# Linear attention into a tanh-shrink MLP on one core: accumulators in one PSUM tile, 1/den of batch 1 spread by TensorE, transposes of batch 2 on TensorE, loads at chunk edges

## The chip, the core and the metric

The kernel runs on one core of a Trainium2 chip. The core's engines work side by side, each with a queue of its own: TensorE (PE, matrix products, with a row of its own in the profile for its weight loads, PEld), VectorE (DVE), ScalarE (ACT), GpSimd (POOL) and SyncE (SP). POOL and SP issue the DMAs here. The metric is the device time of one execution in microseconds (us), the median over runs.

## The reference, cut to what matters

```python
batch, n_heads, seq, head_dim = (8, 8, 576, 64)      # q, k, v
n_tokens, d_model, d_ff = (4608, 512, 2048)          # w_in, w_out

def phi(x):
    return np.where(x > 0, x, np.exp(x) - 1.0) + 1.0
q_p, k_p = (phi(q), phi(k))
kv = np.einsum('bhsd,bhse->bhde', k_p, v)
z = np.sum(k_p, axis=2)
num = np.einsum('bhsd,bhde->bhse', q_p, kv)
den = np.einsum('bhsd,bhd->bhs', q_p, z)[..., None] + 1e-06
attn = (num / den)
x = attn.transpose(0, 2, 1, 3).reshape(B * S, H * D)
h = x @ w_in
g = h - np.tanh(h)
return (g @ w_out)
```

Inputs and output are fp32; products are computed from bf16 with fp32 sums.

## The kernel before

The 4608 tokens are worked on in nine chunks of 512, the loop over `c` at L312. A chunk has two layers. Layer 1 is 16 groups `fi`: four matmuls (`l1mm`, L227) sum one accumulator `h` of 128 x 512, then `l1act` takes a tanh on ACT (L232) and the subtraction on DVE (L233), which writes `gT`. Layer 2 is 16 steps `s` of four matmuls each (`l2mm`, L242) into four accumulators `o`; each, once complete, is copied to SBUF by ACT (L247) and written out by two DMAs on SP (L250). In chunk 0 layer 2 goes over quarters of `gT` first (its four accumulators are open side by side), in all others over accumulators.

Attention is worked on by batch (576 tokens, 8 heads), one batch ahead of the chunk that needs it. Its steps for batch b: load k, q and v by POOL (`load_kq`, `load_v`); `phi` in halves `i`, an exp on ACT (L101) and two operations on DVE (L102, L103), for k (`a_kphi`) and q (`a_qphi`); qT, the transpose of phi(q); the KV products and the sum of k (`a_kv`, 36 matmuls, L142, then a mask on DVE, L146); the denominators (`a_den`, L154 on PE, L158 and L160 on DVE); the spread of 1/den over the 64 rows of each head; the numerators (`num_mm`, L179 and L182) and their product with 1/den, which is x, transposed, in `xT`.

qT is made in two ways. `a_qT_pe` transposes 128 x 128 blocks on PE (L126) and copies them out on ACT and DVE (L130, L132); it serves batches 0 and 1. `a_qT_dma` issues one DMA transpose on SP (L116); it serves the others. 1/den is spread in two ways too. `a_spread` writes it to DRAM (`ds`, four DMAs, L167) and reads it back in broadcast (`rdb`, two DMAs, L170), all on SP; DVE then multiplies numerators in PSUM by `rdb` (`a_num`, L190, L195). It serves batches 1 to 7. For batch 0, `a_num_copy` copies the numerators to SBUF on ACT (L203, L206), `a_spread_pe` spreads 1/den by matmuls with a 0/1 matrix `sel` (L215) into a four-bank accumulator `bp`, and `a_scale` multiplies on DVE (L220).

The order on each engine is that in which the code is written (`manual_schedule`). What of the next batches is put behind which group or step stands in the lists `s1` and `s2` (L315 to L349). Numbers that matter here: in chunk 1, KV of batch 2 behind group 6 and its denominators behind group 15; in chunks 2 to 6, KV behind group 6 and denominators behind group 10; numerators behind steps 9 to 13. Loads of k and q for batch c + 2 are held back by `gate`, a one-element copy on POOL that waits for a group of `gT`: group 11 in chunk 1, group 4 after that.

PSUM is eight banks, handed out by pools: at the start four banks for warm-up and `bp` and four for the rest, from chunk 0 on six (`dps`) for `h` and `o`, and two (`aps`) for attention.

Of the kernel before, what the change touches and what calls it, by code (L numbers as in the profile page):

```python
# [15 lines left out]
def kernel(  # L16
# [27 lines left out]
    opool = ctx.enter_context(tc.tile_pool(name="opool", bufs=5))  # L44
    ctx.enter_context(tc.manual_schedule())

# [73 lines left out]
    def a_qT_pe(b, i, pool, tag):  # L120
        if i == 0:
            new_qT(b)
        for n, (j0, j1) in enumerate(((0, 5), (5, 9))):
            ps = pool.tile([128, 8, 128], BF16, name="tps", tag=tag)
            for j in range(j0, j1):
                nc.tensor.transpose(ps[:, j - j0, :], qp_t[b][:, i, j].rearrange("p h d -> p (h d)"), ident)  # L126
            src = ps[:, 0:j1 - j0, :]
            dst = qT_t[b][:, i, j0:j1].rearrange("p j g t -> p j (g t)")
            if n == 0:
                nc.scalar.copy(dst, src)  # L130
            else:
                nc.vector.tensor_copy(dst, src)  # L132

    def a_kv(b, pool, tag):
        kz_t[b] = work.tile([128, 2, 2, 160], BF16, name="kz")
        kp, vt = kp_t[b], v_b[b % 2]
        ps = [pool.tile([128, 2, 192], F32, name=f"kvps{hg}", tag=tag) for hg in range(2)]
# [10 lines left out]
    def a_den(b, pool, tag):  # L148

        kz, qT = kz_t[b], qT_t[b]  # L150
        ps = pool.tile([128, J, 16], F32, name="denps", tag=tag)
# [6 lines left out]
        nc.vector.tensor_scalar(den, ps.rearrange("p j t -> p (j t)"), 1e-6, None, ALU.add)  # L158
# [16 lines left out]
    def num_mm(b, p, pool, tag):  # L175
        kz, qT = kz_t[b], qT_t[b]
        ps = pool.tile([128, 8, 64], F32, name="numps", tag=tag)
# [8 lines left out]
    def a_num(b, p):  # L186
        rdb = rdb_t[b]
        ps = num_mm(b, p, aps, "aps")
# [10 lines left out]
    def a_num_copy(b, pool, tag):  # L199

        ns = rpool.tile([128, NP, J, 64], F32, name="ns", tag="rdb")
        ps = num_mm(b, NP, pool, tag)
        nc.scalar.copy(ns[:, :, 8, :], ps[:, 0:NP, :])  # L203
        for p in range(NP):
            ps = num_mm(b, p, pool, tag)
            nc.scalar.copy(ns[:, p, 0:8, :], ps)  # L206
# [79 lines left out]
    with tc.tile_pool(name="bpa", bufs=1, space=bass.MemoryType.PSUM) as bpa:  # L286
        with tc.tile_pool(name="sps", bufs=4, space=bass.MemoryType.PSUM) as sps:

            wps = bpa.tile([128, 4, 512], F32, name="wps", tag="bp")
            for n in range(28):  # L290
                nc.tensor.matmul(wps[:, n % 4, :], zero[:, 0:128], zero, start=True, stop=True)
            for i in range(2):
                a_kphi(0, i)
            for i in range(2):
                a_qphi(0, i)
            for i in range(2):
                a_qT_pe(0, i, sps, "sps")
            a_kv(0, sps, "sps")
            a_den(0, sps, "sps")
            ns0 = a_num_copy(0, sps, "sps")  # L300
# [11 lines left out]
    for c in range(NC):  # L312
# [4 lines left out]
        if c == 0:  # L317
            s1[11].append(lambda: a_kphi(1, 0))
# [3 lines left out]
            s2[4].append(lambda: a_qT_pe(1, 0, aps, "aps"))  # L322
            s2[5].append(lambda: a_qT_pe(1, 1, aps, "aps"))
            s2[6].append(lambda: a_kv(1, aps, "aps"))
# [25 lines left out]
        if c == 0:  # L350

            hs = [dps.tile([128, 512], F32, name="h", tag="dps") for _ in range(4)]
# [5 lines left out]
        for fi in range(4 if c == 0 else 0, NF):  # L358
            h = dps.tile([128, 512], F32, name="h", tag="dps")
# [46 lines left out]
```

## Time and profile before

| | |
|---|---|
| three runs | 326.29, 329.56 (median), 329.67 us |
| the profiled execution | 328.22 us |
| its span in the profile | 326.4 us |
| mean granted TensorE clock | 0.961 |
| PE busy, share of the span | 293.0 us, 90% |
| DVE | 180.5 us, 55% |
| ACT | 146.3 us, 45% |
| POOL | 50.6 us, 16% |

The span is what the trace covers; the execution's own time is 1.8 us longer. Times in the views count from the span's start. Busy shares are averages over stages with different limits, so the views to read here are the strip of busy tenths, which shows where PE has holes, PE's waits, which name what ended them, and the chain of waits, which gives the order in time. A granted clock under 1 in a window means that PE ran slower there than it can.

### The profile page before, as it was taken

How to read it: one execution, taken by the hardware profiler on the slowest of the kernel's cores; microseconds unless marked ns; L12 is line 12 of the kernel's file. 1: busy time of each engine (PE TensorE's matmuls, PEld its weight loads, DVE VectorE, ACT ScalarE, POOL GpSimd, SP SyncE). 2: the span in 40 equal slices, each digit the busy share in tenths (PEclk: the TensorE clock that was granted, in tenths of full speed). 3: DMA queues.
4: the chain of work that ended last, by engine and by line, in shares of the span. 5: the costliest groups of instructions: out<-in, count | busy, mean ns of one | idle time of the engine just before them, and what ended most of it. 6: DMA issues, size and time to landing. Idle time of an engine off the chain costs nothing.

```text
span 326.4 us, 4546 instructions
## 1 busy us (share of the span) xinstructions
PE 293.0 (90%) x1698; PEld 138.3 (42%) x1728; DVE 180.5 (55%) x299; ACT 146.3 (45%) x223; POOL 50.6 (16%) x88
## 2 busy tenths in 40 slices
PE   8469999089599999899999998999999999999994
PEld 3334454035233454345444443444454444444441
DVE  5763962069625676557665765586478048405700
ACT  3524842047416456345635562556256126316511
POOL 8924062002300060006000500020000000000000
PEclk9898999759969999999999999999999999999998
DMA  7999999632987678938892979196610730031022
GB/s 113 175 207 202 202 176 171 183 93 35 142 148 180 133 113 138 238 81 128 160 215 66 155 132 241 41 146 167 150 33 4 190 71 15 0 92 38 0 64 64
DMA packets 38901, 40.00 MB, mean 123 GB/s; under 512 B 16768, under 2 KB 33376, under 8 KB 37984
## 3 DMA queue, kind: packets, MB, share of 16 engines
q0 software_dynamic: 17536, 18.35, 35.6%
q1 hardware_dynamic: 21344, 21.37, 29.2%
q8 instruction: 13, 0.21, 0.3%
q14 instruction: 8, 0.07, 0.1%
HBM read 44.96 MB, written 9.57 MB: 167 GB/s over the span
## 4 chain that ended last, share of the span: by engine, by line
PE 65%; DMA 22%; DVE 5%; SPq 2%; issue 2%; ACT 2%; POOL 1%; DVEq 0%; ACTq 0%; POOLq 0%
PE h L227 33%; PE o L242 24%; DMA rdb<-ds 10%; DMA ds<-rden 5%; PE kvps L142 4%; DMA qT<-qp 3%; DMA qraw<-in_q_dram 2%; DMA out_dram<-osb 2%; PE numps L179 2%; DVE rden L160 2%; SPq L167 1%; DVE xT L190 1%; ACT osb L247 1%; PE denps L154 1%; DVE xT L220 1%
## 5 line engine op out<-in xcount | busy, mean ns | idle before, releaser
L242 PE MATMUL o<-w_out_sb,gT 128*128 128x512 bf16 x562 | 132.8, 386 | 1.0 <-issue 0.4
L227 PE MATMUL h<-xT,w_in_sb 128*128 128x512 bf16 x560 | 128.7, 385 | 2.8 <-DVE xT L220 2.0
L233 DVE TENSOR_TENSOR gT<-h,th 128x512 bf16<-128x512 f32 x144 | 97.1, 688 | 55.3 <-ACT th L232 54.7
L232 ACT ACTIVATE th<-h 128x512 f32<-128x512 f32 x144 | 85.2, 598 | 53.6 <-PE h L227 49.9
L242 PEld LDWEIGHTS <-gT 128*128 128x128 bf16 x576 | 56.4, 99 | 83.4 <-issue 20.5
L227 PEld LDWEIGHTS <-w_in_sb 128*128 128x128 bf16 x576 | 56.0, 99 | 70.8 <-issue 6.9
L247 ACT COPY osb<-o 128x512 f32<-128x512 f32 x36 | 21.1, 586 | 108.6 <-PE o L242 83.7
L190 DVE TENSOR_TENSOR xT<-numps,rdb 128x512 bf16<-128x512 f32 x28 | 18.6, 688 | 31.7 <-DMA rdb<-ds 19.7
L179 PE MATMUL numps<-qT,kz 128*128 128x512 bf16 x32 | 12.1, 393 | 14.6 <-DVE xT L190 14.5
L78 POOL DMA_DIRECT2D v<-in_v_dram x32 | 19.3, 638 | 33.9 <-PE kvps L142 25.9
L103 DVE TENSOR_TENSOR kp<-e,r 128x1152 bf16<-128x1152 bf16 x16 | 12.4, 775 | 18.3 <-ACT e L101 17.4
L101 ACT ACTIVATE e<-kraw 128x1152 bf16<-128x1152 bf16 x16 | 18.5, 1161 | 4.5 <-DMA kraw<-in_k_dram 4.5
L101 ACT ACTIVATE e<-qraw 128x1152 bf16<-128x1152 bf16 x16 | 18.4, 1164 | 1.6 <-DMA qraw<-in_q_dram 1.6
L238 POOL COPY g<-gT 1x1 bf16<-1x1 bf16 x5 | 0.9, 178 | 110.7 <-DVE gT L233 110.7
L103 DVE TENSOR_TENSOR qp<-e,r 128x1152 bf16<-128x1152 bf16 x16 | 12.1, 758 | 5.8 <-ACT e L101 4.7
L142 PE MATMUL kvps<-v,kp 64*128 64x192 bf16 x288 | 14.5, 257 | 0.3
L142 PEld LDWEIGHTS <-kp 64*128 64x128 bf16 x288 | 12.5, 100 | 3.4 <-issue 3.2
L63 POOL DMA_DIRECT2D kraw<-in_k_dram x16 | 10.1, 639 | 12.2 <-ACT th L232 9.6
L146 DVE TENSOR_TENSOR kz<-kvps,mask 128x320 bf16<-128x320 f32 (+1 forms) x18 | 7.2, 448 | 5.8 <-PE kvps L142 5.8
L63 POOL DMA_DIRECT2D qraw<-in_q_dram x16 | 10.0, 647 | 2.4 <-issue 2.4
L102 DVE TENSOR_SCALAR r<-kraw 128x1152 bf16<-128x1152 bf16 x16 | 8.0, 503 | 1.9 <-DMA kraw<-in_k_dram 1.9
L160 DVE RECIPROCAL rden<-den 128x144 f32<-128x144 f32 x8 | 8.4, 1053 | 0.3
(36 smaller groups left out, 71.8 us busy)
## 6 DMA issues: line engine op xcount, KB each, us to landing
out_dram<-osb SPq DMA_DIRECT2D x72, 128.0 KB
rdb<-ds SPq DMA_DIRECT2D x14, 576.0 KB
kraw<-in_k_dram POOLq DMA_DIRECT2D x16, 288.0 KB, 5.1
qraw<-in_q_dram POOLq DMA_DIRECT2D x16, 288.0 KB, 7.1
v<-in_v_dram POOLq DMA_DIRECT2D x32, 144.0 KB, 7.6
w_in_sb<-in_moe_w_in_dram POOLq DMA_DIRECT2D x4, 512.0 KB, 8.1
w_out_sb<-in_moe_w_out_dram POOLq DMA_DIRECT2D x4, 512.0 KB, 14.7
ds<-rden SPq DMA_DIRECT2D x28, 4.5 KB
```

The source lines that it names most:

```text
L63: nc.gpsimd.dma_start(out=t[64 * hg:64 * hg + 64].rearrange("p i h j d -> p (i h) (j d)"), in_=src[b, 4 * hg:4 * hg + 4].rearrange("h (p j ...
L78: nc.gpsimd.dma_start(out=v_b[b % 2][64 * hg:64 * hg + 64, i, 0:2].rearrange("p h j d -> p h (j d)"), in_=v[b, h0:h0 + 2].rearrange("h (p ...
L101: nc.scalar.activation(e, x, AF.Exp)
L103: nc.vector.tensor_tensor(store[b][:, i].rearrange("p j h d -> p h j d"), e, r, ALU.min)
L142: nc.tensor.matmul(ps[hg][:, i, :], kp[r, i, j].rearrange("p h d -> p (h d)"), vt[r, i, :, j, :], start=(j == 0), stop=(j == J - 1))
L179: nc.tensor.matmul(ps, kz[:, p // 2, p % 2, 0:128], qT[:, p % 2, 0:8, p // 2, :], start=True, stop=True)
L190: nc.vector.tensor_mul(xT[:, p, S * b:S * b + 512].rearrange("p (j t c) -> p j t c", j=8, t=4), ps.rearrange("p j (t c) -> p j t c", t=4), ...
L227: nc.tensor.matmul(h, w_in_sb[:, p, fi * 128:(fi + 1) * 128], xT[:, p, c * 512:(c + 1) * 512], start=(p == 0), stop=(p == NP - 1))
L232: nc.scalar.activation(th, h, AF.Tanh)
L233: nc.vector.tensor_sub(gT[:, fi, :], h, th)
L242: nc.tensor.matmul(o, gT[:, fi, i * 128:(i + 1) * 128], w_out_sb[:, fi, :], start=(fi == 0), stop=(fi == NF - 1))
L247: nc.scalar.copy(osb, o)
```

## The change

Five things are changed.

1. PSUM is one tile `ps_all` of eight banks. `Banks` gives banks out in a written cycle: 0 to 5 for `h` and `o` (`dense`), 6 and 7 for attention (`attn`), other cycles at the start and in chunk 0, where layer 1 uses all eight and attention uses 4 to 7 in layer 2.
2. The warm-up is 44 matmuls and not 28. At the start both halves of the spread stand ahead of the scales, each with four banks of its own.
3. Batch 1's 1/den is spread on PE: numerators behind step 9 of chunk 0, copied out by ACT, the spread in halves behind steps 11 and 13, each followed by two scales.
4. Batch 2's qT is made on PE, behind groups 5 and 6 of chunk 1. Its phi moves up: k behind steps 14 and 15 of chunk 0, q behind groups 0 and 2 of chunk 1. KV of batch 2 stands behind group 8, its denominators behind group 11. In chunks 2 to 6, KV stands behind group 5 and denominators behind group 8.
5. k and q of batch 3 are loaded behind group 2 of chunk 1, without a gate; those of later batches behind group 0 of their chunk, gated to that group; v behind group 8.

```diff
+    psum = ctx.enter_context(tc.tile_pool(name="psum", bufs=1, space=bass.MemoryType.PSUM))
+    ps_all = psum.tile([128, 8, 512], F32, name="ps_all")
+    class Banks:
+        def __init__(self, order):
+            self.order, self.n = order, 0
+        def __call__(self):
+            self.n += 1
+            return ps_all[:, self.order[(self.n - 1) % len(self.order)], :]
+    dense = Banks([0, 1, 2, 3, 4, 5])
+    attn = Banks([6, 7])
...
-            ps = pool.tile([128, 8, 128], BF16, name="tps", tag=tag)
+            ps = banks().bitcast(BF16).rearrange("p (j t) -> p j t", t=128)
...
-    def a_spread_pe(b, pool, pairs):
+    def a_spread_pe(b, bank0, pairs):
-        bp = pool.tile([128, 4, 512], F32, name="bp", tag="bp")
+        bp = ps_all[:, bank0:bank0 + 4, :]
...
-            for n in range(28):
-                nc.tensor.matmul(wps[:, n % 4, :], zero[:, 0:128], zero, start=True, stop=True)
+    for n in range(44):
+        nc.tensor.matmul(ps_all[:, n % 4, :], zero[:, 0:128], zero, start=True, stop=True)
...
-            bp_a = a_spread_pe(0, bpa, (0, 1))
-        with tc.tile_pool(name="bpb", bufs=1, space=bass.MemoryType.PSUM) as bpb:
-            bp_b = a_spread_pe(0, bpb, (2, 3))
-            for p in range(NP):
-                a_scale(0, p, ns0, (bp_a, bp_b)[p // 2], 144 * (p % 2))
-    dps = ctx.enter_context(tc.tile_pool(name="dps", bufs=6, space=bass.MemoryType.PSUM))
-    aps = ctx.enter_context(tc.tile_pool(name="aps", bufs=2, space=bass.MemoryType.PSUM))
+    bp_a = a_spread_pe(0, 0, (0, 1))
+    bp_b = a_spread_pe(0, 4, (2, 3))
+    for p in range(NP):
+        a_scale(0, p, ns0, (bp_a, bp_b)[p // 2], 144 * (p % 2))
...
+            side = Banks([4, 5, 6, 7])
+            sub = {}
+            def spread1(h):
+                sub["bp"] = a_spread_pe(1, 4, (2 * h, 2 * h + 1))
+                for p in (2 * h, 2 * h + 1):
+                    a_scale(1, p, sub["ns"], sub["bp"], 144 * (p % 2))
...
-            s2[8].append(lambda: (a_den(1, aps, "aps"), a_spread(1)))
-            s2[9].append(lambda: load_v(3))
-            for p in range(NP + 1):
-                s2[min(12 + p, 15)].append(lambda p=p: a_num(1, p))
-            s2[15].append(lambda: a_kphi(2, 0))
+            s2[8].append(lambda: a_den(1, side))
+            s2[9].append(lambda: (sub.update(ns=a_num_copy(1, side)), load_v(3)))
+            s2[11].append(lambda: spread1(0))
+            s2[13].append(lambda: spread1(1))
+            s2[14].append(lambda: a_kphi(2, 0))
+            s2[15].append(lambda: a_kphi(2, 1))
         elif n1 < B:
-            s1[6].append(lambda: a_kv(n1, aps, "aps"))
-            s1[15 if c == 1 else 10].append(lambda: (a_den(n1, aps, "aps"), a_spread(n1)))
+            s1[8 if c == 1 else 5].append(lambda: a_kv(n1, attn))
+            s1[11 if c == 1 else 8].append(lambda: (a_den(n1, attn), a_spread(n1)))
...
-                s1[6].append(lambda: load_v(c + 3))
+                s1[8].append(lambda: load_v(c + 3))
         if c == 1:
-            s1[0].append(lambda: a_kphi(2, 1))
-            s1[2].append(lambda: a_qphi(2, 0))
-            s1[4].append(lambda: (a_qphi(2, 1), a_qT_dma(2)))
+            s1[0].append(lambda: a_qphi(2, 0))
+            s1[2].append(lambda: (a_qphi(2, 1), load_k(3), load_q(3)))
+            s1[5].append(lambda: a_qT_pe(2, 0, attn))
+            s1[6].append(lambda: a_qT_pe(2, 1, attn))
         if c >= 1 and n2 < B:
-            l = 11 if c == 1 else 4
-            s1[l].append(lambda: (gate(gT, l), load_k(n2), load_q(n2)))
-            d = 5 if c == 1 else 2
+            if c > 1:
+                s1[0].append(lambda: (gate(gT, 0), load_k(n2), load_q(n2)))
+            d = 4 if c == 1 else 2
...
-            hs = [dps.tile([128, 512], F32, name="h", tag="dps") for _ in range(4)]
+            hs = [ps_all[:, fi, :] for fi in range(4)]
+            first = Banks([4, 5, 6, 7, 0, 1, 2, 3])
...
-            h = dps.tile([128, 512], F32, name="h", tag="dps")
+            h = first() if c == 0 else dense()
...
-                os_[i] = dps.tile([128, 512], F32, name="o", tag="dps")
+                os_[i] = ps_all[:, i, :] if c == 0 else dense()
```

DVE's rows from the denominators of batch 1, in layer 2 of chunk 0, to the first phi of batch 2. Before:

```order
L158 TENSOR_SCALAR den<-denps 128x144
L160 RECIPROCAL rden<-den 128x144
L190 TENSOR_TENSOR xT<-numps,rdb 128x512 x4
L195 TENSOR_TENSOR xT<-numps,rdb 128x4x64
L102 TENSOR_SCALAR r<-kraw 128x1152
L103 TENSOR_TENSOR kp<-e,r 128x2x9x64
```

And now:

```order
L172 TENSOR_SCALAR den<-ps_all 128x144
L174 RECIPROCAL rden<-den 128x144
L234 TENSOR_TENSOR xT<-ns,ps_all 128x4x9x16 x4
L116 TENSOR_SCALAR r<-kraw 128x1152
L117 TENSOR_TENSOR kp<-e,r 128x2x9x64
```

Five products with `rdb`, which comes from DRAM, are replaced by four scales that read `ns` and the spread in PSUM.

DVE's rows in layer 1 of chunk 1, from the second half of phi(q) of batch 2 on (`gT` rows are the subtractions of layer 1). Before:

```order
L102 TENSOR_SCALAR r<-qraw 128x1152
L103 TENSOR_TENSOR qp<-e,r 128x2x9x64
L233 TENSOR_TENSOR gT<-h,th 128x512 x2
L146 TENSOR_TENSOR kz<-kvps_797,mask 128x320
L146 TENSOR_TENSOR kz<-kvps_798,mask 128x320
L233 TENSOR_TENSOR gT<-h,th 128x512 x9
```

And now:

```order
L116 TENSOR_SCALAR r<-qraw 128x1152
L117 TENSOR_TENSOR qp<-e,r 128x2x9x64
L247 TENSOR_TENSOR gT<-ps_all,th 128x512 x3
L146 COPY qT<-ps_all 128x512
L247 TENSOR_TENSOR gT<-ps_all,th 128x512
```

Two qT copies come in, the first behind three subtractions, the second behind one more. The rows on ACT are alike: tanh of groups 3 to 5 stand between the last exp of q and its first qT copy.

POOL's loads from v of batch 3 to k and q of batch 3. Before:

```order
L78 DMA v_88<-in_v_dram 64x2x576 x4
L78 DMA v_87<-in_v_dram 64x2x576 x4
L238 COPY g_881<-gT 1x1
L63 DMA kraw<-in_k_dram 64x4x576 x2
L63 DMA qraw<-in_q_dram 64x4x576 x2
```

And now, as far as the gate of batch 4's:

```order
L92 DMA v_92<-in_v_dram 64x2x576 x4
L77 DMA kraw<-in_k_dram 64x4x576 x2
L77 DMA qraw<-in_q_dram 64x4x576 x2
L92 DMA v_91<-in_v_dram 64x2x576 x4
L252 COPY g_1043<-gT 1x1
```

k and q of batch 3 move ahead of v of batch 4, and the gate ahead of them is gone; the gate that follows is that of batch 4's k and q.

More of the change, by code (lines that the diff above doesn't have):

```diff
@@ L118, in a_qT_dma, with a_qT_pe @@
             in_=qp_t[b].rearrange("p i j h d -> p (i j h d)"))
-    def a_qT_pe(b, i, pool, tag):
+    def a_qT_pe(b, i, banks):
         if i == 0:
@@ L132, in a_qT_pe, with a_kv @@
                 nc.vector.tensor_copy(dst, src)
-    def a_kv(b, pool, tag):
+    def a_kv(b, banks):
         kz_t[b] = work.tile([128, 2, 2, 160], BF16, name="kz")
         kp, vt = kp_t[b], v_b[b % 2]
-        ps = [pool.tile([128, 2, 192], F32, name=f"kvps{hg}", tag=tag) for hg in range(2)]
+        ps = [banks()[:, 0:384].rearrange("p (i e) -> p i e", i=2) for hg in range(2)]
         for i in range(2):
@@ L146, in a_kv, with a_den @@
                 nc.vector.tensor_mul(kz_t[b][:, hg, i, :], ps[hg][:, i, 0:160], mask[:, hg, i, :])
-    def a_den(b, pool, tag):
+    def a_den(b, banks):
         kz, qT = kz_t[b], qT_t[b]
-        ps = pool.tile([128, J, 16], F32, name="denps", tag=tag)
+        ps = banks()[:, 0:J * 16]
         for n, p in enumerate((0, 2, 1, 3)):
@@ L173, in a_spread, with num_mm @@
         rdb_t[b] = rdb
-    def num_mm(b, p, pool, tag):
+    def num_mm(b, p, banks):
         kz, qT = kz_t[b], qT_t[b]
-        ps = pool.tile([128, 8, 64], F32, name="numps", tag=tag)
+        ps = banks().rearrange("p (j t) -> p j t", j=8)
         if p < NP:
@@ L284 @@
         nc.vector.memset(v_b[i][:, :, 2], 1.0)
[L286 to L307 removed]
+    for n in range(44):
+        nc.tensor.matmul(ps_all[:, n % 4, :], zero[:, 0:128], zero, start=True, stop=True)
+    for i in range(2):
+        a_kphi(0, i)
+    for i in range(2):
+        a_qphi(0, i)
+    first = Banks([4, 5, 6, 7, 0, 1, 2, 3])
+    for i in range(2):
+        a_qT_pe(0, i, first)
+    a_kv(0, first)
+    a_den(0, first)
+    ns0 = a_num_copy(0, first)
+    bp_a = a_spread_pe(0, 0, (0, 1))
+    bp_b = a_spread_pe(0, 4, (2, 3))
+    for p in range(NP):
+        a_scale(0, p, ns0, (bp_a, bp_b)[p // 2], 144 * (p % 2))
     load_k(2)
```

17 lines of the change are left out of this document (9 added, 8 removed).

## The prediction

> **What bounds the kernel now.** I read the page's strip of busy tenths first, then TensorE's (PE's) waits, then the chain of waits in order of time, and last the timeline of the places these name. In the page's two strips, 40 slices of 8.16 us each, the reader is to see that PE is full from the twelfth slice on, and that its holes and its low granted clock lie together in the first third.
>
> ```profile
> PE   8469999089599999899999998999999999999994
> ...
> PEclk9898999759969999999999999999999999999998
> ```
>
> PE's waits (total us, times, longest) name the holes: numerators that wait for VectorE (DVE) to free an accumulator, one of them 10.2 us long; the denominators of batch 2 behind a DMA transpose; transposes at the start.
>
> ```profile
> PE numps L179 <- DVE xT L190: 14.5, 6, 10.2
> PE tps L126 <- DVE qp L103: 4.5, 2, 3.9
> PE denps L154 <- DMA qT<-qp: 3.5, 1, 3.5
> PE h L227 <- DVE xT L220: 2.0, 1, 2.0
> ```
>
> The chain (start, duration, what) gives each chunk's first layer-1 matmul:
>
> ```profile
> 24.49 0.59 PE h L227
> ...
> 69.74 4.25 PE h L227 x14
> ...
> 109.34 6.04 PE h L227 x28
> ...
> 141.54 5.83 PE h L227 x27
> ...
> 172.96 6.04 PE h L227 x28
> ...
> 205.20 5.83 PE h L227 x27
> ...
> 235.97 6.04 PE h L227 x28
> ```
>
> So chunk 0 takes 45.25 us, chunk 1 39.60, chunks 2 to 4 32.20, 31.42 and 32.24, and chunk 5, without a wait, 30.77. A 512-column matmul costs 6.04 / 28 = 0.216 us, a group of four 0.86, one layer of 64 13.8. PE is the bound; what the change can win is the distance of chunks 0 to 4, and of the start, from 30.8.
>
> **The start.** The timeline ahead of chunk 0 (start, duration, engine, line; in brackets the idle time before):
>
> ```profile
> 1.19 7.50 PE L291 MATMUL wps<-zero 128*128 128x512 bf16 x28 [1.19 <-DVE zero L254]
> ...
> 13.88 1.00 PE L126 MATMUL tps<-ident,qp 128*128 128x128 bf16 x9 [0.61 <-DVE qp L103]
> ...
> 14.82 2.93 PE L142 MATMUL kvps<-v,kp 64*128 64x192 bf16 x36
> ...
> 17.79 1.02 DVE L146 TENSOR_TENSOR kz<-kvps,mask 128x160 bf16<-128x160 f32 x4 [2.43 <-PE kvps L142]
> ...
> 19.50 1.05 DVE L160 RECIPROCAL rden<-den 128x144 f32<-128x144 f32 x1
> 19.63 2.06 ACT L206 COPY ns<-numps 128x512 f32<-128x512 f32 x4
> ...
> 21.60 2.75 DVE L220 TENSOR_TENSOR xT<-ns,bp 128x576 bf16<-128x576 f32 x4 [1.05 <-PE bp L215]
> 21.75 0.77 PE L215 MATMUL bp<-rden,sel 32*128 32x144 f32 x16 [0.28 <-ACT ns L206]
> ...
> 24.49 0.59 PE L227 MATMUL h<-xT,w_in_sb 128*128 128x512 bf16 x1 [1.97 <-DVE xT L220]
> ```
>
> and the window behind it, with its granted clock (0.57, behind the 3.29 and 8 matmuls):
>
> ```profile
> 24.00:28.00 4.00, 3.29 (x8) 1.29 (x10) 0.34 (x1) 0.00 (x0) 1.19 (x2) 0.57 1.21 207
> ```
>
> The same work at full clock, from chunk 0 (nine transposes, the KV products, the denominators), and the round trip of batch 1's 1/den through DRAM, from its first issue on SP to the product that uses it:
>
> ```profile
> 44.36 0.50 PE tps L126 x9
> ...
> 47.09 1.59 PE kvps L142 x36
> ...
> 50.52 0.39 PE denps L154 x16
> ...
> 52.36 0.35 SPq L167
> ...
> 66.06 0.70 DVE xT L190
> ```
>
> Sixteen more warm-up matmuls at 0.216 end at about 12.1 instead of 8.69. They delay nothing, since q arrives later than that, and the 3.9 us hole ahead of the transposes shrinks to half a us. I take the clock as full from there: transposes at 13.88 for 0.50, KV for 1.59, so KV ends at 16.0 instead of 17.75, and kz, den and rden move up by 1.75. The scales start at 19.85. Layer 1 needs no longer all four of them but two (its first four banks are those that the first two read), 1.4 us: it starts at 21.4 instead of 24.49. Price of the slow window: 3.5 us of PE hold 16 matmuls at 0.216, and 8 ran, so 1.7 us. If the start stays at a low clock, 1.7 comes back; if all four scales are still waited for, 1.3.
>
> **Chunk 0.** Removed: six DMAs (four ds, two rdb) on SP, with their 13.7 us from 52.36 to 66.06 that PE waits out, and five products on DVE. Added: five copies on ScalarE (ACT) (the 2.06 row's four, and a half-size one), two spreads on PE (0.77 each, the L215 row) and four scales (2.75 / 4 each) on DVE. ACT and DVE are free there, since layer 2 gives them only four evacuations. From 21.4: layer 1 13.8; layer 2 13.8; 18 transposes 1.0; KV 1.6; den 0.4; numerators 1.0 (four at 0.216, four of 64 columns 0.1); spreads 1.5; two short waits, 0.2 for the bank of the fourth numerator (its ACT copy) and 0.3 for the last copy ahead of the first spread (2.45 us of copies against two steps and the numerators, 2.7). Sum 33.6: chunk 1 starts at 55.0 instead of 69.74, **14.7 us less**. The spread's second half comes two steps (1.73) after the first, and the two scales that it waits for take 1.4: no wait. Loads are not late by this: they stand in the same order on POOL as far as batch 2.
>
> **Chunk 1.** The DMA transpose and its 3.5 us wait go; 18 PE transposes come into layer 1, behind groups 5 and 6. Their inputs come late. From chunk 1 as it is (and the two qT copies from chunk 0):
>
> ```profile
> 74.09 1.16 ACT L101 ACTIVATE e<-qraw 128x1152 bf16<-128x1152 bf16 x1
> 75.14 1.08 ACT L232 ACTIVATE th<-h 128x512 f32<-128x512 f32 x2
> 75.15 0.45 DVE L102 TENSOR_SCALAR r<-qraw 128x1152 bf16<-128x1152 bf16 x1
> 75.70 0.76 DVE L103 TENSOR_TENSOR qp<-e,r 128x1152 bf16<-128x1152 bf16 x1
> 76.38 1.28 DVE L233 TENSOR_TENSOR gT<-h,th 128x512 bf16<-128x512 f32 x2
> ...
> 44.68 0.69 ACT L130 COPY qT<-tps 128x640 bf16<-128x640 bf16 x1 [1.29 <-PE tps L126]
> ...
> 45.19 0.42 DVE L132 COPY qT<-tps 128x512 bf16<-128x512 bf16 x1
> ```
>
> By starts, an exp costs ACT 1.05, a tanh 0.54; r and min cost DVE 1.23, a subtraction 0.60 to 0.64. Counting from the chunk's first matmul: ACT has one k exp, the last evacuation and the other k exp until 2.5, tanh 0 until 3.05, a q exp until 4.1, tanh 1 and 2, the other q exp until 6.25, tanh 3 to 5 until 7.85, and only then the first qT copy, until 8.45. DVE, in its written order, ends subtraction 0 at 4.1, q half 0 at 5.3, subtractions 1 and 2 at 6.6, q half 1 at 7.8, subtractions 3 to 5 at 9.6, its qT copy at 10.0. PE does groups 0 to 5 until 5.2, waits 0.2, transposes until 5.9, does group 6 until 6.8. Half 1's first five transposes need bank 6, so ACT's copy (8.45); its last four need bank 7, so DVE's (10.0). They end at 10.4 instead of 7.1: **a new wait of 3.3 us**. Behind PE stand all later groups. Bounds: nothing, if ACT and DVE are ahead, to 4.5 at the isolated durations in place of the spacing by starts.
>
> Gaps of 0.5, 0.3 and 2.0 us ahead of 24.49 sufficed for the 0.57; here 1.8 and 1.2 us stand close together, so I count 1.7 of slow clock behind them. Chunk 1: 30.8 + 1.0 + 3.3 + 1.7 = 36.8 instead of 39.6, **2.8 less**. The Trainium skill ("TensorE: Matmul & The Clock Gate", section "Why this matters for your kernels") says that gaps up to about 3 us between bursts keep the clock; by it the 1.7 would not come, and the total be 305.5. The 1.97 row ahead of the 0.57 window speaks against it. The Trainium skill, in the same "TensorE: Matmul & The Clock Gate", section "Part 4: PE-mode transpose", puts a transpose at about 275 ns; by it, batch 2's 18 would cost 5.0, not 1.0, and the total be 311. The trace disagrees: nine in 0.50 us.
>
> **Chunks 2 to 4.** Denominators move from behind group 10 to behind group 8, 1.73 us earlier, and the waits to win there are 1.43, 0.65 and 1.47: all go, **3.5 less**. k and q are loaded from the chunk's first group on, ahead of the round trip. SP's rows of chunk 2 and of chunk 5, which loads no v:
>
> ```profile
> 123.22 1.29 SPq L167 DMA_DIRECT2D ds<-rden  x4
> 128.14 1.12 SPq L170 DMA_DIRECT2D rdb<-ds  x2
> ...
> 219.08 1.33 SPq L167 DMA_DIRECT2D ds<-rden  x4
> 221.47 1.12 SPq L170 DMA_DIRECT2D rdb<-ds  x2
> ```
>
> ds to rdb takes 4.92 with loads under way and 2.39 without, so the gating gives 0 to 2.5 us of slack, which nothing then waits for. In chunk 1 the path from den to the third numerator on PE is 4 groups, 12 steps and two numerators, 14.3; against it stand some 2.5 on DVE (a subtraction ahead, den, rden), the round trip's 13.7 less 2.5 for the loads, and a product, 14.4: a tie, at most 1 us. The one PSUM tile adds no instruction; PE's rows show waits by bank, and runs of layer-1 matmuls without any.
>
> **Sum.** 14.7 + 2.8 + 3.5 = 21.0 off the profiled execution's 328.2: 307. That execution is 1.3 below the median of the three runs, so 308 against the median; I keep 307, inside the runs' own spread.
>
> **Rivals.** (a) Chunk 1's wait costs less: the clock stays up (305.5), or ACT and DVE are also ahead (302). For it: each single gap is under 2 us. Against: the order on ACT and DVE. 0.22. (b) More stays: the start at low clock again, 1.7, and waits of chunks 2 to 4, 3.5, because the round trip grows with what is loaded: 309 to 313. For it: the two spreads, 1.5 us, are nearly all that PE has in the three us ahead of 21.4. 0.20. (c) Slower: the one tile is waited for as a whole, not by bank, so that layer 1's next group waits until ACT and DVE have read the last. At 0.54 + 0.64 for each of 144 groups 170 us, so near 480. It decides from 21 / 144 = 0.15 us a group. Against it stand PE's rows. 0.03. (d) The change doesn't do what it says in chunk 0: the hole is filled only in part, because copies, spreads and scales queue on ACT and DVE; over 313. 0.05. My forecast, 303.5 to 311 around 307: 0.50.
>
> **Chances.** About 1% can be told from no change here, since the three runs span 1%. Faster by over that: all but (c) and a little of (d), 0.95; within 0.02; slower 0.03. The range takes in (a) and (b): 302 to 313.
>
> **What would show it.** Right: no ds or rdb before chunk 1, whose first matmul stands near 55; KV products at the start in 1.6 us; layer 1 at 21.4; a wait of PE for the qT copies of about 3 us in chunk 1, with a low clock behind it; chunks 2 to 4 at 30.8. Wrong: a wait for bp or ns in chunk 0, a low clock at 24, or numps still waiting for xT in chunks 2 to 4.

## The result, and the profile after

| | before | after |
|---|---|---|
| median (runs) | 328.94 us (4; 326.29 to 329.67) | 307.72 us (4; 307.01 to 309.31) |
| the profiled execution, its span | 328.22, 326.4 us | 307.01, 305.2 us |
| mean granted TensorE clock | 0.961 | 0.991 |
| PE busy, share of the span | 293.0 us, 90% | 295.0 us, 97% |

The ratio is 0.9375, with a 95% interval of 0.9307 to 0.9443: the change is 6.3% faster. PE is busy 2.0 us longer than before and has 23 us fewer holes.

The first view is again the strip of busy tenths and granted clock, here of the kernel after, in slices of 7.63 us:

```profile
PE   8979999969999999999999999999999999999993
...
PEclk9999999979999999999999999999999999999998
```

The wide hole of chunk 0 is gone. Between the start and the end one slice is left below 9, the ninth (61 to 69 us), and the low clock lies in the same slice. PE's waits of the kernel after (us in total, times, longest) name it:

```profile
PE ps_all L140 <- ACT qT L144: 1.4, 1, 1.4
...
PE ps_all L140 <- DVE qT L146: 1.2, 1, 1.2
PE ps_all L241 <- DVE xT L234: 0.6, 1, 0.6
PE ps_all L229 <- DVE rden L174: 0.5, 1, 0.5
```

The first two are the wait that the prediction announced, transposes that wait until the qT copies have freed their banks. There is no wait of numerators for `xT` any more (14.5 us before), none for a DMA transpose (3.5), and in this execution no transpose waits for `qp` (4.5; in e10, the same kernel run again, 1.1). In chunk 0 the two halves of batch 1's spread stand among layer 2's matmuls, with no wait in brackets:

```profile
49.95 0.77 PE L229 MATMUL ps_all<-rden,sel 32*128 32x144 f32 x16
...
52.48 0.77 PE L229 MATMUL ps_all<-rden,sel 32*128 32x144 f32 x16
```

The chain in order of time (start, duration, what) and PE's timeline give the chunks' first layer-1 matmuls; the first fence is the chain, the second the timeline, both of the kernel after:

```profile
21.53 13.97 PE ps_all L241 x64
...
91.24 5.18 PE ps_all L241 x24
...
122.01 5.18 PE ps_all L241 x24
...
152.79 5.18 PE ps_all L241 x24
...
183.56 5.18 PE ps_all L241 x24
```

```profile
1.19 12.11 PE L302 MATMUL ps_all<-zero 128*128 128x512 bf16 x44 [1.19 <-DVE zero L268]
13.13 1.43 PE L140 MATMUL ps_all<-ident,qp 128*128 128x128 bf16 x18
...
14.49 1.66 PE L156 MATMUL ps_all<-v,kp 64*128 64x192 bf16 x36
...
21.53 2.75 PE L241 MATMUL ps_all<-xT,w_in_sb 128*128 128x512 bf16 x12 [0.63 <-DVE xT L234]
...
54.92 5.34 PE L241 MATMUL ps_all<-xT,w_in_sb 128*128 128x512 bf16 x24
```

The chain's starts lie up to 0.2 behind those of the timeline (in both kernels), so the lengths below are taken from the timelines of both:

| | before | after | less |
|---|---|---|---|
| layer 1 of chunk 0 starts | 24.49 | 21.53 | 3.0 |
| chunk 0 | 45.06 | 33.39 | 11.7 |
| chunk 1 | 39.63 | 36.15 | 3.5 |
| chunks 2 to 4 | 32.19, 31.42, 32.24 | 30.78, 30.78, 30.77 | 3.5 |

That is 21.7; the last chunk, from its first matmul to the end of the span, takes 0.4 more (32.66 for 32.21), and the span is 21.2 shorter.

### The profile page after: what moved, and what is told of

The parts are those of the page before. It is cut to its first block, busy times and chain, and to the rows that moved or that the text cites. A ratio compares the mean times of both kernels' runs of the same rounds, so it can differ in the third digit from the quotient of the medians.

```text
span 305.2 us, 4703 instructions
## 1 busy us (share of the span) xinstructions
PE 295.0 (97%) x1794; PEld 139.9 (46%) x1794; DVE 181.1 (59%) x300; ACT 149.5 (49%) x230; POOL 50.4 (17%) x87
## 4 chain that ended last, share of the span: by engine, by line
PE 86%; DVE 5%; DMA 4%; ACT 2%; issue 1%; SPq 0%; POOL 0%; DVEq 0%; ACTq 0%; POOLq 0%
PE ps_all L241 40%; PE ps_all L256 37%; PE ps_all L156 4%; DMA out_dram<-osb 2%; PE ps_all L193 2%; ACT e L115 2%; DMA kraw<-in_k_dram 2%; DVE gT L247 1%; PE ps_all L168 1%; DVE qp L117 1%; ACT osb L261 1%; DVE kp L117 1%; PE ps_all L229 1%; PE ps_all L140 1%; DVE r L116 1%
## 5 line engine op out<-in xcount | busy, mean ns | idle before, releaser
L256 PE MATMUL ps_all<-w_out_sb,gT 128*128 128x512 bf16 x576 | 131.6, 379 | 0.0
L241 PE MATMUL ps_all<-xT,w_in_sb 128*128 128x512 bf16 x576 | 129.4, 382 | 0.6 <-DVE xT L234 0.6
L247 DVE TENSOR_TENSOR gT<-ps_all,th 128x512 bf16<-128x512 f32 x144 | 96.9, 686 | 55.6 <-ACT th L246 55.1
L246 ACT ACTIVATE th<-ps_all 128x512 f32<-128x512 f32 x144 | 85.1, 598 | 54.0 <-PE ps_all L241 49.4
L261 ACT COPY osb<-ps_all 128x512 f32<-128x512 f32 x36 | 21.1, 585 | 79.7 <-PE ps_all L256 59.6
L204 DVE TENSOR_TENSOR xT<-ps_all,rdb 128x512 bf16<-128x512 f32 x24 | 16.4, 689 | 11.8 <-PE ps_all L193 11.8
L92 POOL DMA_DIRECT2D v<-in_v_dram x32 | 19.1, 615 | 21.2 <-PE ps_all L156 9.0
L117 DVE TENSOR_TENSOR qp<-e,r 128x1152 bf16<-128x1152 bf16 x16 | 12.1, 758 | 6.9 <-ACT e L115 5.9
L156 PE MATMUL ps_all<-v,kp 64*128 64x192 bf16 x288 | 13.3, 243 | 0.0
L302 PE MATMUL ps_all<-zero 128*128 128x512 bf16 x44 | 12.1, 446 | 1.2 <-DVE zero L268 1.2
L193 PE MATMUL ps_all<-qT,kz 128*128 128x512 bf16 x32 | 11.2, 379 | 0.0
L160 DVE TENSOR_TENSOR kz<-ps_all,mask 128x320 bf16<-128x320 f32 (+1 forms) x18 | 7.2, 448 | 4.9 <-PE ps_all L156 4.9
```

What stands on the lines that cost most here:

```text
L92: nc.gpsimd.dma_start(out=v_b[b % 2][64 * hg:64 * hg + 64, i, 0:2].rearrange("p h j d -> p h (j d)"), in_=v[b, h0:h0 + 2].rearrange("h (p ...
L117: nc.vector.tensor_tensor(store[b][:, i].rearrange("p j h d -> p h j d"), e, r, ALU.min)
L156: nc.tensor.matmul(ps[hg][:, i, :], kp[r, i, j].rearrange("p h d -> p (h d)"), vt[r, i, :, j, :], start=(j == 0), stop=(j == J - 1))
L193: nc.tensor.matmul(ps, kz[:, p // 2, p % 2, 0:128], qT[:, p % 2, 0:8, p // 2, :], start=True, stop=True)
L204: nc.vector.tensor_mul(xT[:, p, S * b:S * b + 512].rearrange("p (j t c) -> p j t c", j=8, t=4), ps.rearrange("p j (t c) -> p j t c", t=4), ...
L241: nc.tensor.matmul(h, w_in_sb[:, p, fi * 128:(fi + 1) * 128], xT[:, p, c * 512:(c + 1) * 512], start=(p == 0), stop=(p == NP - 1))
```

## The experiments

Ten kernels, one of them run twice (e4 and e11), in three groups, each group beside runs of the kernel before on its chip (medians 329.45, 329.70 and 330.27 us; 328.94 beside the change). e10 is the change itself, run again beside the last group. "Above" and "below the change" are counted from its 307.72; since the medians of the kernel before differ by 1.3 us, smaller differences are not told apart.

**Batch 1's spread, undone** (e3). Its 1/den goes through DRAM again, everything else stays:

```diff
-            s2[8].append(lambda: a_den(1, side))
-            s2[9].append(lambda: (sub.update(ns=a_num_copy(1, side)), load_v(3)))
-            s2[11].append(lambda: spread1(0))
-            s2[13].append(lambda: spread1(1))
+            s2[8].append(lambda: (a_den(1, side), a_spread(1)))
+            s2[9].append(lambda: load_v(3))
+            for p in range(NP + 1):
+                s2[min(12 + p, 15)].append(lambda p=p: a_num(1, p))
```

> Batch 1's 1/den through DRAM again, numerators multiplied behind steps 12 to 15 of chunk 0; all else as in the change. Theory: the hole of about 10 us ahead of chunk 1 and the low clock behind it are back, chunk 1 starts near 65 and not 54.9, the time rises by 11, to 318 to 319. Rival (half of the 14.4 us that chunk 1 starts earlier came from the start and from eight banks in layer 1, and the hole shrinks since loads are done earlier): 312 to 315.

Measured: 315.34 us (314.88 to 315.80), ratio 0.9561 [0.9518, 0.9604]; 7.6 above the change. Its timeline on ACT and PE (start, duration, engine, line; idle time before in brackets):

```profile
52.57 1.17 ACT L115 ACTIVATE e<-kraw 128x1152 bf16<-128x1152 bf16 x1
...
62.95 0.58 PE L193 MATMUL ps_all<-qT,kz 128*128 128x512 bf16 x1 [10.90 <-DVE xT L204]
...
65.69 5.81 PE L241 MATMUL ps_all<-xT,w_in_sb 128*128 128x512 bf16 x24
...
74.39 0.38 PE L140 MATMUL ps_all<-ident,qp 128*128 128x128 bf16 x4 [0.96 <-DVE qT L146]
```

The hole is back with its 10.9 us, and chunk 1 starts 10.8 later (65.69 for 54.92). But chunk 1 then takes 33.65 and not 36.15: its wait for qT is 1.0 instead of 2.6, and no low clock follows it. ACT did the first exp of batch 2's k at 52.57, inside the hole, 13.1 us ahead of chunk 1; in the change that exp starts at 54.74, 0.2 ahead of it. So the hole had a use: in it ACT got one exp ahead (DVE was idle in it). Filling it gains 10.8 at once and gives 2.5 back in chunk 1. So the expected 318 to 319 were missed by 3, although the hole came as the theory has it. The rival's 312 to 315 come close, but not by its reason: the hole did not shrink.

**Batch 2's transposes, undone** (e2). qT of batch 2 by DMA again, with chunk 1's old places for phi, KV, denominators and loads:

```diff
-            s2[14].append(lambda: a_kphi(2, 0))
-            s2[15].append(lambda: a_kphi(2, 1))
+            s2[15].append(lambda: a_kphi(2, 0))
...
-            s1[8 if c == 1 else 5].append(lambda: a_kv(n1, attn))
-            s1[11 if c == 1 else 8].append(lambda: (a_den(n1, attn), a_spread(n1)))
+            s1[6 if c == 1 else 5].append(lambda: a_kv(n1, attn))
+            s1[15 if c == 1 else 8].append(lambda: (a_den(n1, attn), a_spread(n1)))
...
-            s1[0].append(lambda: a_qphi(2, 0))
-            s1[2].append(lambda: (a_qphi(2, 1), load_k(3), load_q(3)))
-            s1[5].append(lambda: a_qT_pe(2, 0, attn))
-            s1[6].append(lambda: a_qT_pe(2, 1, attn))
+            s1[0].append(lambda: a_kphi(2, 1))
+            s1[2].append(lambda: a_qphi(2, 0))
+            s1[4].append(lambda: (a_qphi(2, 1), a_qT_dma(2)))
...
```

> Batch 2's qT by DMA transpose again, with chunk 1's old order, its old gate and its old places for KV and denominators; all else as in the change. Theory (this part was worth 2.8 us, since a wait of 3.5 for the DMA transpose went and one of 2.6 for the copies came): chunk 1 takes 38.5 us, the 39.6 of before less 1.1 of low clock at its start that the filled hole no longer causes; the time rises by about 2.2, to 310. Rival (the part gave nothing): 307 to 308. Rival (the part gave all of chunk 1's gain and more, since the loads now collide with the transpose): over 312.

Measured: 311.47 us (310.49 to 311.70), ratio 0.9437 [0.9384, 0.9489]; 3.7 above the change. Chunk 1 takes 39.64, not the expected 38.5. Its timeline on PE and, below it, a window of its clock (the columns are explained in the last section) show why:

```profile
72.96 0.43 PE L168 MATMUL ps_all<-qT,kz 128*32 128x144 bf16 x16 [1.40 <-DMA qT<-qp]
...
89.93 0.58 PE L193 MATMUL ps_all<-qT,kz 128*128 128x512 bf16 x1 [5.64 <-DVE xT L204]
```

```profile
89.76:93.18 3.42, 3.25 (x8) 1.13 (x8) 3.21 (x7) 0.00 (x0) 0.00 (x0) 0.50 0.02 9
```

The DMA transpose costs only 1.4 here, but with the denominators behind group 15 the round trip of 1/den comes late and costs 5.6, and another 1.6 by the half clock behind that wait (3.25 us busy at 0.50). What the transposes on PE buy is, as I read it, above all that the denominators can stand behind group 11: there, four groups (3.5 us) earlier, they would have waited some 4.9 us for e2's DMA transpose (an estimate, 1.4 + 3.5). The run puts back phi, KV, denominators and loads together, so this is not shown by itself. The change has no wait at all for `xT` in chunk 1, so the round trip fits there.

**phi of batch 2 earlier** (e1). If the new wait comes from ACT and DVE being late with phi, moving phi up, and the second half's transposes one group later, should remove it:

```diff
-            s2[14].append(lambda: a_kphi(2, 0))
-            s2[15].append(lambda: a_kphi(2, 1))
+            s2[11].append(lambda: a_kphi(2, 0))
+            s2[13].append(lambda: a_kphi(2, 1))
+            s2[14].append(lambda: a_qphi(2, 0))
+            s2[15].append(lambda: a_qphi(2, 1))
...
-            s1[0].append(lambda: a_qphi(2, 0))
-            s1[2].append(lambda: (a_qphi(2, 1), load_k(3), load_q(3)))
+            s1[2].append(lambda: (load_k(3), load_q(3)))
...
-            s1[6].append(lambda: a_qT_pe(2, 1, attn))
+            s1[7].append(lambda: a_qT_pe(2, 1, attn))
```

> All four phi halves of batch 2 move into layer 2 of chunk 0 (k behind steps 11 and 13, q behind 14 and 15), and the second half's transposes stand one group later. Theory (the 2.6 us that PE waits in chunk 1 are the qT copies, queued on ScalarE and VectorE behind late exps and subtractions): PE waits for them 0.9 us or less, no slow clock window follows in chunk 1, chunk 1 takes 32 to 33 us and not 36.3, and the time falls by about 4, to 303 to 304. Rival (the copies are late whatever stands ahead of them, or the exps now delay the scales and evacuations of chunk 0 by as much): the time stays at 306 to 309.

Measured: 303.36 us (303.02 to 305.06), ratio 0.9208 [0.9160, 0.9256], the fastest kernel of the case, 4.4 below the change. Its timeline on PE and DVE:

```profile
56.95 5.34 PE L241 MATMUL ps_all<-xT,w_in_sb 128*128 128x512 bf16 x24
...
62.12 0.67 PE L140 MATMUL ps_all<-ident,qp 128*128 128x128 bf16 x9
...
64.24 0.41 DVE L146 COPY qT<-ps_all 128x512 bf16<-128x512 bf16 x1
64.35 0.73 PE L140 MATMUL ps_all<-ident,qp 128*128 128x128 bf16 x9
```

Neither row of transposes has a wait in brackets, and chunk 1 takes 32.21. Its profiled execution is the slowest of the four (305.06): it lost about 1.7 to a low clock behind the start, which the section on the hardware comes back to.

**Filling the wait** (e8). Twelve matmuls with the zero tile into an idle bank, ahead of the second half's transposes, keep PE busy while it waits. They separate the low clock from the wait itself:

```diff
+            def filler():
+                for n in range(12):
+                    nc.tensor.matmul(ps_all[:, 1, :], zero[:, 0:128], zero, start=True, stop=True)
-            s1[6].append(lambda: a_qT_pe(2, 1, attn))
+            s1[6].append(lambda: (filler(), a_qT_pe(2, 1, attn)))
```

> Twelve matmuls of zeros, 2.6 us, into the bank that group 7 overwrites next, put ahead of the second half's transposes in chunk 1, where PE now waits 2.6 us for qT copies. Theory (1.7 us of what that wait costs are the slow clock behind it): they run inside the wait, PE waits 0.5 or less for qT, no slow window follows, chunk 1 takes 34.6 us and not 36.3, the time falls by 1.7. Rival (the clock falls for another reason, or does not count): no change. Rival (they lie on the path): 2.6 more.

Measured: 306.01 us (305.94, 305.99, 306.04), clocks 1.000, 1.000 and 0.997, ratio 0.9270 [0.9217, 0.9323]; 1.7 below the change. The profiled execution took 801 us, so its trace isn't read, and that the matmuls lay inside the wait rests on the times and clocks alone. The price of the clock can also be read without e8: e6 and e7, below, leave chunk 1 as it is and have the same two waits, but kept the clock behind them, and their chunk 1 takes 34.76 and 34.79 us instead of 36.15 (36.39 in e10).

**Chunks 2 to 4: which edit carries them?** Denominators back behind group 10 (e5), loads back to their old places (e6), both (e7):

```diff
-            s1[8 if c == 1 else 5].append(lambda: a_kv(n1, attn))
-            s1[11 if c == 1 else 8].append(lambda: (a_den(n1, attn), a_spread(n1)))
+            s1[8 if c == 1 else 6].append(lambda: a_kv(n1, attn))
+            s1[11 if c == 1 else 10].append(lambda: (a_den(n1, attn), a_spread(n1)))
```

```diff
-                s1[8].append(lambda: load_v(c + 3))
+                s1[8 if c == 1 else 6].append(lambda: load_v(c + 3))
...
-                s1[0].append(lambda: (gate(gT, 0), load_k(n2), load_q(n2)))
+                s1[4].append(lambda: (gate(gT, 4), load_k(n2), load_q(n2)))
```

The first diff alone:

> In chunks 2 to 6 KV stands behind group 6 and denominators behind group 10 again, with the new places of the loads kept. In the change's chunk 2, ds goes out at 103.39, rdb at 106.71, and the third numerator runs at 117.4, some 2.3 us after its accumulator could be free (8.1 for the rdb landing and 0.7 for the product counted from 106.71). Theory (earlier denominators and loads at the chunk's edge each cover the 0.65 to 1.47 us by themselves): 1.73 us later still fits, chunks 2 to 4 stay at 30.8, the time stays within 0.5 of the change. Rival (the earlier denominators carry it, the loads do nothing): chunks 2 to 4 grow by up to 1.5 each, 3.5 in all.

The second alone:

> In chunks 2 to 6 k and q are loaded behind group 4 and v behind group 6 again, with the new places of KV and denominators kept. Theory: ds to rdb grows from 3.3 to 4 to 5 us, which the 2.3 us of slack hold, so chunks 2 to 4 stay at 30.8 and the time stays within 0.5 of the change. Rival (the loads' place carries it): up to 3.5 more.

Both:

> Both at once: KV, denominators and loads of chunks 2 to 6 in the places of before. Theory: 1.73 and 1.6 together exceed 2.3, the waits of before come back, chunks 2 to 4 take 32.2, 31.4 and 32.2, and the time rises by 3 to 3.5. Rival (the gain of chunks 2 to 4 came from chunk 1's end, out of whose way later chunks start): no change.

| | median (us) | ratio | chunks 2, 3, 4 | ds to rdb in chunk 2 |
|---|---|---|---|---|
| the change | 307.72 | 0.9375 | 30.78, 30.78, 30.77 | 3.32 |
| e5, denominators late | 306.79 | 0.9297 [0.9244, 0.9349] | 30.77, 30.78, 30.78 | 2.33 |
| e6, loads late | 308.03 | 0.9333 [0.9279, 0.9387] | 30.77, 30.95, 31.72 | 5.76 |
| e7, both | 312.09 | 0.9473 [0.9405, 0.9541] | 32.55, 32.49, 31.94 | 4.89 |

The last column is the time from the first issue of `ds` to the first of `rdb` on SP. SP's rows in chunk 2, of e5 first, then of e7:

```profile
105.59 1.29 SPq L181 DMA_DIRECT2D ds<-rden  x4
107.92 1.55 SPq L184 DMA_DIRECT2D rdb<-ds  x2
```

```profile
104.71 1.29 SPq L181 DMA_DIRECT2D ds<-rden  x4
109.60 1.11 SPq L184 DMA_DIRECT2D rdb<-ds  x2
```

and the wait of PE that e7 has again and e5 has not:

```profile
PE ps_all L193 <- DVE xT L204: 4.6, 3, 1.8
```

The last load of the chunk, v, is issued by POOL ahead of `ds`, and the time from `ds` to `rdb` is the longer the closer it stands. POOL's rows, of e5 first, then of e7:

```profile
98.90 2.39 POOL L92 DMA_DIRECT2D v<-in_v_dram  x4 [1.92 <-PE ps_all L156]
```

```profile
99.49 2.43 POOL L92 DMA_DIRECT2D v<-in_v_dram  x4
```

They end 4.3 us ahead of `ds` in e5 and 2.8 in e7; it is 3.5 in the change and 1.1 in e6. In the order of this distance (e5, the change, e7, e6), `ds` to `rdb` takes 2.33, 3.32, 4.89 and 5.76.

Denominators two groups later cost nothing as long as the loads are early: the theory held for e5's chunks. Its median lies 0.9 below the change's; two of its four executions kept the clock (0.997; 305.92 and 306.12), and none of the change's first four did (0.986 to 0.993). Late loads cost 1.1 us over three chunks if the denominators are early, where none was expected (e6's time stays within the expected 0.5). Both together cost 4.7, where 3 to 3.5 were expected: all that chunks 2 to 4 had gained and 1.2 more. Either edit nearly suffices; the change makes both.

**The start.** 28 warm-up matmuls instead of 44 (e4, and with more runs e11), and none (e12; its diff takes the loop out):

```diff
-    for n in range(44):
+    for n in range(28):
```

> 28 warm-up matmuls in place of 44; all else as in the change. Theory (the clock falls in the hole ahead of the transposes, and KV on the path is then slow): KV of batch 0 takes 2.9 us and not 1.66, layer 1 starts 1.7 us later, and the time rises by 1.8, by up to 3.5 if the clock is low at the start of layer 1 too. Rival (the start is bound by loads and VectorE, not by PE's clock): no change, within 0.5.

> 28 warm-up matmuls again, since three rounds left it open (308.26 against 307.72, single times from 306.67 to 311.06, and 2.4 us more until layer 1 in its profile). Theory (a free-running window decides whether the 3.6 us hole lowers the clock, so the cost is 2.4 in some executions and little in others): the median is 0.5 to 2.4 above the change's, and the times spread more widely. Rival (the 16 added matmuls do nothing): medians within 0.3, equal spread.

> No warm-up matmuls at all. Theory (transposes and KV of batch 0 then run at half clock in every execution): layer 1 starts at 24 to 24.5 and not at 21.5, and every time is 2.4 or more above the change's, without the spread that 28 show; more by up to 1.7 where layer 1 starts at half clock too. Rival (the start is bound by loads and VectorE): within 0.5 of the change.

> The change as it is, timed beside the next two runs on the same chip: 307 to 309.

| | median (us), runs | layer 1 starts |
|---|---|---|
| e10, 44, the change again | 307.50 (306.07 to 308.39), 6 | 21.70 |
| e4, 28 | 308.26 (306.67 to 311.06), 4 | 23.93 |
| e11, 28 | 309.16 (307.71 to 310.31), 6 | 23.39 |
| e12, none | 307.65 (307.12 to 310.08), 6 | 23.74 |

e4 is within its own spread of the change. e11's median is 1.65 above that of e10, as expected, but its times spread no more widely. PE's timeline of e11:

```profile
1.19 8.20 PE L302 MATMUL ps_all<-zero 128*128 128x512 bf16 x28 [1.19 <-DVE zero L268]
12.63 2.39 PE L140 MATMUL ps_all<-ident,qp 128*128 128x128 bf16 x18 [3.24 <-DVE qp L117]
14.95 3.06 PE L156 MATMUL ps_all<-v,kp 64*128 64x192 bf16 x36
...
23.39 4.91 PE L241 MATMUL ps_all<-xT,w_in_sb 128*128 128x512 bf16 x22 [0.63 <-DVE xT L234]
```

With 28, PE idles 3.2 us, the KV products take 3.06 instead of 1.66, and layer 1 starts 1.7 later than in e10, near the 1.65 between the medians. These starts are of one execution each; among eight profiled executions with 44 (the change, e10, e1 to e3 and e5 to e7) layer 1 starts at 21.52 to 22.49. e12 missed its expectation: layer 1 starts 2.0 later in its profile, yet its median is only 0.15 above that of e10. By the granted clock the runs fall in two groups (the start does not count in e12's clock: the record gives 1.00 there, although KV takes 3.06 us):

| | clock 0.997 to 0.998 | clock 0.986 to 0.993 |
|---|---|---|
| e10, 44 | 306.07, 306.86 | 307.40, 307.60, 307.99, 308.39 |
| e12, none | 307.12 to 307.74, four runs | 309.14, 310.08 |

Inside each group no warm-up costs about 1 to 2 us; the medians come together because four of six runs of the change are in the lower group and two of six of e12. One window of 3.41 us at half clock is 3.41 x 0.5 / 305 = 0.006 of the mean clock, the distance of the groups. Whether the start has an influence on how often that window comes, or six runs are too few, stays open.

**The one tile alone** (e9). The change's PSUM tile, banks by hand and its order of the first spread, with 28 warm-up matmuls and the lists `s1` and `s2` of before:

```diff
-    for n in range(44):
+    for n in range(28):
...
-            s2[11].append(lambda: spread1(0))
-            s2[13].append(lambda: spread1(1))
+            for p in range(NP + 1):
+                s2[min(12 + p, 15)].append(lambda p=p: a_num(1, p))
...
-            s1[5].append(lambda: a_qT_pe(2, 0, attn))
-            s1[6].append(lambda: a_qT_pe(2, 1, attn))
+            s1[4].append(lambda: (a_qphi(2, 1), a_qT_dma(2)))
...
```

> The kernel before with only PSUM changed to the one tile and banks by hand (0 to 5 for h and o, 6 and 7 for attention; 28 warm-ups, all orders, loads and transposes as before). Theory (the tile adds no wait by itself; at the start layer 1 waits for two scales and not for four): the start gains 1.2 to 1.4 us, all chunks stay as before, the time is 327.5 to 328.5 against 329.5. Rival (part of the 14.4 us by which chunk 1 starts earlier came from the banks): chunk 0 shorter by more than 2. Rival (waits for the whole tile): far slower.

Measured: 327.51 us (325.30 to 328.67), ratio 0.9909 [0.9872, 0.9945]; 2.8 below before. PE's timeline:

```profile
22.82 5.56 PE L241 MATMUL ps_all<-xT,w_in_sb 128*128 128x512 bf16 x25 [0.63 <-DVE xT L234]
```

Layer 1 starts 1.7 earlier than in the kernel before. 1.3 of it is the idle time ahead of it, 0.63 instead of 1.97, because its banks do not wait for the last scales; the rest is no more than starts differ between executions. Its 64 matmuls then take 13.81 instead of 15.39, since no low clock follows; that is in part chance, since e1, with the same 0.63, had a low clock there. Chunk 0 takes 43.53 for 45.06, so the first rival (more than 2 from the banks) did not come, and all other chunks take about what they took before (40.09, 32.03, 31.31, 32.36 for chunks 1 to 4). The tile adds no wait.

## Why the prediction was right

307.0 was forecast, within 302 to 313, and 307.72 measured. That the total agrees to 0.2 us (21.0 forecast, 21.2 between the profiled spans) has some luck in it: chunk 1 gained 3.5 for the 2.8 forecast, and the last chunk lost 0.4 that stands in no term. By its steps:

- **The start.** Layer 1 at 21.4 was forecast and 21.53 measured; the KV products end at 16.15 (forecast 16.0), and no low clock follows at 24 (in e1, whose start is the same, one does). One term inside was off: the 44 matmuls were to end at 12.1 and end at 13.3, because in this execution the clock rose later, at 6.16 and not at 3.83 (there the spacing of the warm-up matmuls goes from 0.427 to 0.216 us). It cost nothing, since the second half of phi(q) comes at 13.83. Two of the scales suffice for layer 1: it starts at 21.53, while the row of all four, from 20.06, ends at 22.81.
- **Chunk 0.** Chunk 1 at 55.0 was forecast and 54.92 measured. The two short waits (0.2 and 0.3) did not come; the other terms took 0.3 more than their sum (33.39 for 33.1).
- **Chunk 1.** The place, the cause and the low clock behind it were right: the qT copies on ACT and DVE free the banks late, behind tanh and subtractions. The wait was sized too long, 2.6 and not 3.3, and the chunk took 36.15, not 36.8. PE's, ACT's and DVE's timeline of the change:

```profile
59.82 1.19 ACT L115 ACTIVATE e<-qraw 128x1152 bf16<-128x1152 bf16 x1
60.88 1.59 ACT L246 ACTIVATE th<-ps_all 128x512 f32<-128x512 f32 x3
61.79 0.76 DVE L117 TENSOR_TENSOR qp<-e,r 128x1152 bf16<-128x1152 bf16 x1
62.31 0.75 ACT L144 COPY qT<-ps_all 128x640 bf16<-128x640 bf16 x1
62.47 1.88 DVE L247 TENSOR_TENSOR gT<-ps_all,th 128x512 bf16<-128x512 f32 x3
63.11 0.44 PE L140 MATMUL ps_all<-ident,qp 128*128 128x128 bf16 x5 [1.39 <-ACT qT L144]
64.26 0.41 DVE L146 COPY qT<-ps_all 128x512 bf16<-128x512 bf16 x1
64.73 0.58 PE L140 MATMUL ps_all<-ident,qp 128*128 128x128 bf16 x4 [1.18 <-DVE qT L146]
```

  From the chunk's start at 54.92, ACT's copy ends at 8.14 (forecast 8.45) and DVE's at 9.75 (10.0). The rows show the order that the sum went through: three tanh between the exp and ACT's copy, three subtractions between `qp` and DVE's. The clock cost 1.4 and not 1.7 in this execution, since part of the slow window fell into the second wait and PE was busy in 2.87 us of it; e6 and e7, with the clock kept, take 1.4 less. By the starts of PE's rows the two waits delay it by 2.9 (2.6 in brackets). 30.8 for the chunk, 1.0 for the transposes, 2.9 for the waits and 1.4 for the clock make 36.1. e1 shows the cause of the wait; e8, e6 and e7 show the price of the clock.
- **The round trip in chunk 1** was called a tie; it has no wait. With the denominators behind group 15 (e2) it costs 5.6, and 1.6 in clock.
- **Chunks 2 to 4.** 3.5 less was forecast and 3.5 measured. That the gating only gives slack was half right: alone it also removes the waits (e5), and where the denominators are early but the loads late, 1.1 comes back (e6).
- **Rival (a)**, a clock that stays up in chunk 1, is what two of six further runs did, by their granted clock of 0.998 (306.07 and 306.86), and what e8 does in each of its three timed runs by theirs. In which stretch a run lost its clock is seen only where it has a trace: in chunk 1 in both of the change. Its other half, no wait at all, is e1: 303.36, where the rival had 302. Of **(b)**, the low clock behind the start came neither in the change nor in e10, but in one (e1) of the eight profiled executions with this start, so that it stayed away here is in part luck; the waits of chunks 2 to 4 did not come. **(d)** did not come, and **(c)** is excluded by e9.

The four parts undone one at a time are worth 7.6 (e3), 3.7 (e2), 4.4 (e7) and 1.65 (e11), the tile alone 2.8 (e9): 20.2 of some 22 (21.2 by the first medians, 22.8 by e10's). That batch 1's spread gives 2.5 back in chunk 1 (e3) would account for such a difference, but no run was made to settle that sum.

## What to carry to other kernels

When a hole of the bounding engine is filled, ask what the other engines did in it: the work that they had got done there (here one exp on ACT) is late in the next stage, and the first copy or transpose that depends on it waits. Where two edits attack the same wait (earlier start, fewer transfers in between), undo each alone and both together; here each alone was nearly free to drop, and both together cost all of the gain. A wait of TensorE of 2.6 us can cost another 1.3 to 1.7 in clock (chunk 1 takes 36.08 to 36.44 us in the six traces that lost it there, 34.76 and 34.79 in the two that kept it), so it is worth filling it with matmuls on a dead bank if it can't be removed.

## What the runs showed of the hardware

The granted clock falls in pieces of 3.41 us, or two or three of them on end, that lie on one grid within an execution: in the kernel before it is low, ahead of the last matmul, for 3.41, 3.41, 10.24 and 6.83 us from 14.07, 24.31, 61.86 and 89.16, and these starts are 3, 11 and 8 times 3.413 us apart. The grid's place differs between executions: the spacing of the warm-up matmuls falls to 0.216 us at 3.83 in the kernel before and at 6.16 after. Ahead of that first rise the record shows 1.00, though the matmuls stand 0.427 us apart. So the clock is read by windows of that grid. The columns are window, length, busy time and instructions of PE, PEld, DVE, ACT and POOL, then the granted clock, DMA share and GB/s. The kernel after in chunk 1:

```profile
60.78:64.19 3.41, 1.38 (x11) 0.62 (x9) 3.31 (x6) 3.22 (x7) 1.22 (x2) 1.00 0.98 136
64.19:67.60 3.41, 2.87 (x10) 1.26 (x10) 1.50 (x4) 0.78 (x2) 0.00 (x0) 0.50 0.98 163
67.60:71.01 3.41, 3.41 (x45) 2.13 (x44) 2.27 (x4) 0.82 (x3) 1.63 (x3) 1.00 0.12 15
```

e6 in chunk 1, with the same two waits (1.38 and 1.19 us), 0.3 us later on the grid:

```profile
60.75:64.16 3.41, 1.72 (x17) 0.96 (x15) 3.31 (x7) 3.21 (x7) 1.22 (x2) 1.00 1.08 154
64.16:67.57 3.41, 2.47 (x23) 1.39 (x25) 2.38 (x5) 1.56 (x3) 0.00 (x0) 1.00 1.00 162
```

PE was busy 1.38 of 3.41 us in the one, and the next window ran at half clock; 1.72 in the other, and the clock stayed up. Among the windows read, the clock fell behind 1.38 and less each time (1.34 in the kernel before, 1.35 in e2, 1.10 in e10) and went both ways between 1.45 and 1.57 (it fell behind 1.49 in e4 and 1.52 in e12; the kernel before stayed up behind 1.45 and 1.57). So two waits of 1.39 and 1.18 us sufficed where 2.03 us of them fell into one window, and the same waits cost up to 1.7 us more in one run than in another. The Trainium skill ("TensorE: Matmul & The Clock Gate", section "What's actually happening") says that the activity window is free-running and 3413 ns long; the trace agrees, with its 3.41. The Trainium skill's rule that the prediction weighed (the same page, section "Why this matters for your kernels"), gaps up to about 3 us, does not hold here: two gaps, each under 1.4 us, lost the clock.

Busy time alone does not decide it. The start of e1, and below it that of e9:

```profile
18.56:21.97 3.41, 2.27 (x35) 1.61 (x34) 2.30 (x4) 1.87 (x4) 0.75 (x1) 1.00 1.23 203
21.97:25.39 3.42, 3.42 (x9) 1.22 (x8) 1.17 (x2) 0.00 (x0) 1.11 (x2) 0.50 1.22 206
```

```profile
19.84:23.25 3.41, 2.27 (x35) 1.70 (x35) 2.30 (x4) 1.54 (x4) 1.00 (x2) 1.00 1.24 208
23.25:26.66 3.41, 3.41 (x17) 1.56 (x16) 1.05 (x3) 0.84 (x2) 0.42 (x1) 1.00 1.21 205
```

PE was busy 2.27 with 35 matmuls in both, mostly the small fp32 ones of the spread, and the clock fell in the one and stayed up in the other. Whether small matmuls count less was not tried; these two windows leave open what decides.
